# Linear attention with a gated feed-forward: the kernel's table of steps replaced by another

## Chip, cores, metric

The kernel runs on one NeuronCore of a Trainium2 chip. The metric is the device time of one execution in microseconds (us); lower is better. Three runs of the kernel before the change gave 242.40, 241.68 and 242.57 us, median 242.4.

## What is computed

Linear attention with phi(x) = elu(x) + 1 over q, k, v of shape (8 batches, 8 heads, 576 positions, 64), then a gated feed-forward over 4608 tokens, all float32 at the borders:

```python
q_p, k_p = (phi(q), phi(k))
kv = np.einsum('bhsd,bhse->bhde', k_p, v)
z = np.sum(k_p, axis=2)
num = np.einsum('bhsd,bhde->bhse', q_p, kv)
den = np.einsum('bhsd,bhd->bhs', q_p, z)[..., None] + 1e-06
attn = num / den
...
x = attn.transpose(0, 2, 1, 3).reshape(4608, 512)
a = x @ w1          # 512 x 1024
b = x @ w2          # 512 x 1024
h = a * b @ w3      # 1024 x 1024
return h @ w_out    # 1024 x 512
```

## The kernel before

**Work.** w3 and w_out are multiplied on the chip once, so that the end of the chain is one product with a 1024 x 512 matrix (wf). The 4608 tokens are 36 tiles of 128; four tiles make a chunk, and there are nine chunks, 0 to 8. Each chunk has eight gate units, one for 128 columns of w1 and w2: four matmuls of 512 columns for a, four for b, a copy of a to SBUF on ScalarE (ACT) and a product with b on VectorE (DVE). An output tile is eight matmuls over the eight units' results.

**Steps.** The program is a table of steps, `ORDER` (lines 21 to 60). Each entry calls one small function (`s_F`, `s_KV`, and so on, lines 133 to 562); the queues of all engines are filled in the order of the table, nothing is reordered afterwards, and an engine works off its queue strictly in that order. The last letter names the engine that copies: a is ACT, v is DVE, p is GpSimd (POOL), s is SyncE (SP). The steps that matter here:

- `LK LQ LV` load half a batch of k, q or v (576 KB); `L3 LH LO LA LB` load pieces of w3, w_out, w1 and w2 (512 KB, `LH` half of it). All these transfers are issued by SP, one after the other. They land in 13 buffers ("ld", line 96) that are given out first in, first out: the 14th load waits until the buffer that was first given back is read.
- `CO CA CB` cast a piece of w_out, w1 or w2 to bf16. `T3` and `C3` turn a block of w3, `FW` adds to wf.
- `EX`, `PT`, `PM` make phi: exp on ACT, max(x,0)+1 and the minimum of the two on DVE. `VC` casts v. `KV` and `KB` make kv for a batch.
- `QP` transposes phi(q) on TensorE (PE) through PSUM, with a copy back; `QD` does it as a DMA transpose between two SBUF tiles (line 385; ACT issues it when the letter is a, else SP).
- `ND` makes one tile of normalised attention: products on PE, then reciprocal and multiplication on DVE. `NT` with three `NM` does it for three tiles with one reciprocal.
- `XP` (PE and a copy) or `XD` (DMA transpose, SP) turn these tiles round for the gate units.
- `F` is a whole gate unit; `FI` one side of it (a or b); `FP` one side for two of the four tiles, in the same PSUM buffer as the other two, which are read together; `FS` one side for two tiles in a PSUM buffer of its own, read by itself as 128x256.
- `O` is an output tile with its copy, `S` its store (two DMAs), `Q` the last tile in pieces.

**PSUM.** Four buffers ("mm") hold gate units and outputs, two ("at") the rest; each is free again when its copy is done.

**Stages.** First wf is made while weights and batch 0 arrive, then chunk 0 goes through its gate units as pieces of w1 and w2 arrive (units 0 to 3 need the first column half, 4 to 7 the second), then chunks follow one another with the output tiles of earlier chunks between them. In SBUF, w1 and w2 are cut as `w_part` says:

```python
    def w_part(w, x):
        if x > 5:
            return w[:, 2 * x - 12:2 * x - 10, 0:NCH]
        if x > 3:
            return w[:, :, P * (x - 4):P * (x - 3)]
        return w[:, :, 256 * x:256 * x + 256] if x < 2 else w[:, 2 * x - 4:2 * x - 2, NCH:DFF]
```

Pieces 6 and 7 are the two row halves of the first 512 columns; pieces 0 and 1 are columns 0 to 255 and 256 to 511 with all rows; 2 and 3 are the row halves of the second 512 columns.

Of the kernel before, what the change touches and what calls it, by code (L numbers as in the profile page):

```python
# [18 lines left out]


ORDER = """
I.0 H.3.0 L3.2 LO.0 I.1 T3.2.0.a H.1.1 CO.0.v FW.2.0.a T3.2.1.a H.1.2 LO.1 CO.1.a L3.4 T3.4.0.v
T3.4.1.v L3.3 T3.3.0.a LO.2 FW.4.0.v FW.4.1.a LO.3 L3.5 T3.3.1.v C3.5.a CO.2.v FW.2.1.a FW.2.2.a
CO.3.v FW.2.3.v L3.6 C3.6.v FW.3.0.a FW.3.1.v LK.0.0 T3.5.0.v LH.0.0 T3.5.1.v LQ.0.0 FW.4.2.v
EX.k.0.0 PT.k.0.0 FW.4.3.a EX.q.0.0 T3.6.0.v PM.k.0.0 FW.5.0.v FW.5.1.v L3.1 T3.6.1.a PT.q.0.0
PM.q.0.0 L3.7 FW.5.2.v FW.6.0.a FW.3.2.a FW.3.3.v FW.5.3.v LQ.0.1 T3.1.0.a C3.7.v T3.1.1.a FW.1.0.v
FW.1.1.a LK.0.1 PT.q.0.1 EX.q.0.1 PM.q.0.1 T3.7.0.a FW.6.1.v FW.6.2.a FW.6.3.a LV.0.0 I.2 T3.0.0.v
LV.0.1 EX.k.0.1 PT.k.0.1 T3.7.1.a LH.0.1 FW.7.0.a FW.7.1.v FW.1.2.v VC.0.0.v QP.0.0.v QP.0.1.a
FW.7.2.a KV.0.0.a PM.k.0.1 VC.0.1.v FW.7.3.v FW.1.3.a KV.0.1.v T3.0.1.a ND.0 FW.0.0.v LA.6 ND.1
FW.0.1.v CA.6.a LA.7 CA.7.a ND.2 FW.0.2.a XP.0.a XP.1.a ND.3 FW.0.3.a FP.0.0.0.0 LB.6 LQ.1.1  # L30
EX.q.1.1 LB.7 LA.3 XP.2.v XP.3.v FP.0.1.0.0 CB.7.a LA.2 FP.0.1.0.1 LB.3 PT.q.1.1 PM.q.1.1 FI.0.2.0
FI.0.3.0 CB.6.v FI.0.1.1 LB.2 CA.2.a LQ.1.0 CB.3.v FP.0.0.0.1 FI.0.0.1 FI.0.3.1 CB.2.v QP.1.1.v
CA.3.a PT.q.1.0 LK.1.0 FI.0.2.1 PT.k.1.0 EX.q.1.0 PM.q.1.0 F.0.4 EX.k.1.0 PM.k.1.0 F.0.5 LV.1.0
VC.1.0.a F.0.6 LK.1.1 EX.k.1.1 PT.k.1.1 PM.k.1.1 LV.1.1 LK.3.0 KV.1.0.a VC.1.1.a F.0.7 LQ.3.1
QP.1.0.a KV.1.1.v PT.k.3.0 EX.q.3.1 EX.k.3.0 O.0.a LQ.3.0 EX.q.3.0 PT.q.3.1 ND.4 ND.5 O.1.a XP.4.a
ND.6 ND.7 PM.k.3.0 LK.2.0 XP.5.a O.2.a PM.q.3.1 XP.6.v XP.7.v LQ.2.1 EX.k.2.0 LQ.2.0 PT.k.2.0
PM.k.2.0 PT.q.3.0 EX.q.2.0 LK.3.1 PM.q.3.0 O.3.a LV.4.1 F.1.0 LV.2.0 LK.4.1 S.0.s F.1.1 PT.q.2.1
EX.q.2.1 S.1.s PT.k.3.1 F.1.2 EX.k.3.1 PM.k.3.1 LK.2.1 PM.q.2.1 F.1.3 VC.2.0.a LV.2.1 PT.k.2.1
PT.q.2.0 PM.q.2.0 EX.k.2.1 F.1.4 LV.3.0 F.1.5 VC.2.1.a PM.k.2.1 F.1.6 LV.3.1 VC.3.0.v QD.2.1
EX.k.4.1 KB.2.a QD.2.0 VC.3.1.a ND.8 QD.3.0 F.1.7 KB.3.a NT.9 NM.9.0 NM.9.1 QD.3.1 XD.2.0 NM.9.2  # L40
XD.2.1 S.2.s LK.4.0 O.4.v O.5.v NT.12 LV.4.0 NM.12.0 O.6.v NM.12.1 O.7.v NM.12.2 LQ.4.1 PT.k.4.0
F.2.0 F.2.1 F.2.2 F.2.3 F.2.4 EX.k.4.0 PT.k.4.1 LQ.5.1 F.2.5 PM.k.4.1 F.2.6 VC.4.0.a LQ.4.0 VC.4.1.a
PM.k.4.0 F.2.7 S.3.s S.4.s LQ.5.0 LK.5.1 PT.q.5.0 EX.q.5.0 NT.15 PM.q.5.0 EX.q.4.1 NM.15.0 PT.q.4.1
PM.q.4.1 PT.q.4.0 LQ.7.1 S.5.s KB.4.a PT.k.5.1 O.8.v EX.k.5.1 S.6.s LK.5.0 EX.k.5.0 PT.k.5.0 XD.3.0
XD.3.1 O.9.a O.10.a O.11.v LV.5.1 F.3.0 PM.k.5.1 LK.6.0 F.3.1 PM.k.5.0 EX.q.4.0 NM.15.1 NM.15.2
LV.5.0 S.7.s S.8.s LK.6.1 F.3.2 S.9.s S.10.s VC.5.0.v PM.q.4.0 QD.4.0 EX.k.6.0 QD.4.1 F.3.3 F.3.4
EX.q.5.1 PT.q.5.1 PM.q.5.1 PT.k.6.1 F.3.5 F.3.6 F.3.7 QD.5.1 O.12.v NT.18 QD.5.0 NM.18.0 XD.4.0
NM.18.1 VC.5.1.a PT.k.6.0 KB.5.a XD.4.1 LQ.6.1 O.13.a O.14.v PT.q.7.1 O.15.v F.4.0 EX.q.7.1 PM.q.7.1
F.4.1 F.4.2 NM.18.2 LK.7.0 F.4.3 NT.21 EX.k.6.1 NM.21.0 NM.21.1 NM.21.2 LV.6.0 VC.6.0.v F.4.4 F.4.5
S.11.s S.12.s PT.k.7.0 LK.7.1 LQ.7.0 F.4.6 LV.6.1 VC.6.1.v S.13.s S.14.s F.4.7 PT.q.7.0 PM.k.6.1  # L50
LQ.6.0 PM.k.6.0 O.16.v EX.q.7.0 O.17.v PM.q.7.0 PT.q.6.1 LV.7.0 O.18.v XD.5.0 XD.5.1 EX.q.6.1
PM.q.6.1 LV.7.1 VC.7.0.a S.15.s EX.q.6.0 KB.6.a NT.24 O.19.v NM.24.0 PT.q.6.0 PM.q.6.0 QD.6.1 F.5.0
VC.7.1.v EX.k.7.1 PT.k.7.1 F.5.1 F.5.2 EX.k.7.0 NM.24.1 NM.24.2 QD.7.1 PM.k.7.0 F.5.3 F.5.4 QD.6.0
PM.k.7.1 F.5.5 S.16.s S.17.s NT.27 XD.6.0 NM.27.0 NM.27.1 QD.7.0 KB.7.a NM.27.2 F.5.6 XD.6.1 XD.7.0
F.5.7 S.18.s NT.30 S.19.s O.20.v S.20.s F.6.0 NM.30.0 NM.30.1 NM.30.2 F.6.1 XD.7.1 O.21.v NT.33
O.22.v NM.33.0 NM.33.1 O.23.v F.6.2 F.6.3 F.6.4 F.6.5 F.6.6 F.6.7 F.7.0 F.7.1 F.7.2 F.7.3 F.7.4
F.7.5 F.7.6 S.21.s S.22.s S.23.s XD.8.0 NM.33.2 XD.8.1 O.24.a O.25.v O.26.v O.27.v S.24.s S.25.s
S.26.s S.27.s F.7.7 F.8.0 F.8.1 F.8.2 F.8.3 F.8.4 F.8.5 F.8.6 F.8.7 O.28.a O.29.a O.30.a S.28.s
S.29.s S.30.s O.31.v S.31.s O.32.v S.32.s O.33.v S.33.s O.34.a S.34.b Q.35
"""  # L60


# [540 lines left out]
```

## Time and profile before

| | |
|---|---|
| median of three runs | 242.4 us (241.68 to 242.57) |
| the profiled execution | 241.85 us, of which 240.1 us from the first to the last instruction (the span) |
| PE busy | 230.6 us, 96% of the span, 2227 matmuls |
| DVE, ACT, POOL busy | 158.2, 113.9, 1.3 us |
| moved by DMA | 55.79 MB; the 16 DMA engines are full for the first 70 us |
| granted TensorE clock | 0.997 |

Times inside the execution count from the first instruction. A matmul's end is modelled, so PE's busy time includes the run-out of each burst. An engine's idle time costs only if the chain that ends last passes through it.

### The profile page before, as it was taken

To read this page: it belongs to the slowest core of one execution; us is meant where nothing else is said; L and a number is where in the kernel's file an instruction comes from. 1 tells how busy PE (TensorE), PEld (TensorE's weight loads), DVE (VectorE), ACT (ScalarE), POOL (GpSimd) and SP (SyncE) were. 2 spreads that over 40 slices of the span, in tenths; PEclk is the share of its full clock that TensorE was granted. 3 is DMA by queue.
4 is the path that set the end of the run, shared out by engine and by line. 5 is a ranking of instruction groups with operands and counts; after the bars stand their busy time and mean duration, and the time that the engine had idled before them with its cause. 6 is when DMAs were issued, how large, how long until landed. Compare 5 with 4: busy or idle time off the path is not lost.

```text
span 240.1 us, 5470 instructions
## 1 busy us (share of the span) xinstructions
PE 230.6 (96%) x2227; PEld 115.8 (48%) x2246; DVE 158.2 (66%) x287; ACT 113.9 (47%) x166; POOL 1.3 (1%) x9
## 2 busy tenths in 40 slices
...
DMA  6999999999998999989959998795653001700276
GB/s 245 418 376 405 387 387 390 388 391 389 397 272 155 183 362 360 319 195 317 257 111 279 381 369 211 123 202 111 137 120 83 3 0 44 163 15 0 45 155 149
DMA packets 52040, 55.79 MB, mean 232 GB/s; under 512 B 31280, under 2 KB 31536, under 8 KB 52016
## 3 DMA queue, kind: packets, MB, share of 16 engines
...
q8 instruction: 17, 0.28, 0.5%
...
## 4 chain that ended last, share of the span: by engine, by line
PE 90%; DMA 5%; DVE 1%; issue 1%; SPq 1%; ACT 0%
PE a_ps L482 26%; PE b_ps L482 26%; PE o_ps L535 24%; PE wf_ps L263 6%; DMA w<-in_moe_w_dram 3%; PE nd L398 2%; DMA qt<-phq 2%; PE w3p L251 2%; PE kbp L340 1%; PE qp L368 1%; PE xp L457 1%; PE kvp L340 1%; DVE w3t L252 1%; SPq L157 1%; DVE xt L458 0%
## 5 line engine op out<-in xcount | busy, mean ns | idle before, releaser
L482 PEld LDWEIGHTS <-w_sb 128*128 128x128 bf16 x584 | 56.4, 98 | 66.9 <-issue 0.9
L491 ACT COPY a_sb<-a_ps 128x512 f32<-128x512 f32 x72 | 42.1, 585 | 80.9 <-PE a_ps L482 79.0
L493 DVE TENSOR_TENSOR ab<-a_sb,b_ps 128x512 bf16<-128x512 f32 x72 | 49.1, 686 | 39.3 <-PE b_ps L482 37.5
L482 PE MATMUL a_ps<-xt,w_sb 128*128 128x512 bf16 (+1 forms) x296 | 74.0, 374 | 0.1
L482 PE MATMUL b_ps<-xt,w_sb 128*128 128x512 bf16 x288 | 73.8, 380 | 0.0
L535 PE MATMUL o_ps<-wf_sb,ab 128*128 128x512 bf16 (+2 forms) x290 | 63.5, 368 | 1.2 <-issue 0.6
L535 PEld LDWEIGHTS <-ab 128*128 128x128 bf16 x304 | 28.3, 98 | 31.2
L542 DVE COPY o_sb<-o_ps 128x512 f32<-128x512 f32 x23 | 15.9, 690 | 20.6 <-PE o_ps L535 19.5
L404 DVE TENSOR_TENSOR xn<-nd,r 128x512 bf16<-128x512 f32 (+2 forms) x45 | 24.3, 578 | 0.5
L273 ACT ACTIVATE eq<-q 128x1152 bf16<-128x1152 f32 x16 | 18.4, 1163 | 6.1 <-DVE phk L293 3.1
L273 ACT ACTIVATE ek<-k 128x1152 bf16<-128x1152 f32 x16 | 18.7, 1167 | 2.0 <-DMA k<-in_k_dram 1.9
L263 PE MATMUL wf_ps<-wo_sb,w3t 128*128 128x512 bf16 x59 | 15.7, 384 | 1.7 <-DVE wo_sb L217 1.0
L542 ACT COPY o_sb<-o_ps 128x512 f32<-128x512 f32 x12 | 7.0, 580 | 15.7 <-PE o_ps L535 15.7
L293 DVE TENSOR_TENSOR phq<-phq,eq 128x1152 bf16<-128x1152 bf16 x16 | 12.0, 752 | 1.4 <-ACT eq L273 0.9
L285 DVE TENSOR_SCALAR phq<-q 128x1152 bf16<-128x1152 f32 x16 | 12.1, 753 | 0.8 <-DMA q<-in_q_dram 0.8
L285 DVE TENSOR_SCALAR phk<-k 128x1152 bf16<-128x1152 f32 x16 | 12.1, 753 | 0.1
L293 DVE TENSOR_TENSOR phk<-phk,ek 128x1152 bf16<-128x1152 bf16 x16 | 12.0, 752 | 0.2
L327 ACT CAST vt<-v 128x1152 bf16<-128x1152 f32 x9 | 10.3, 1159 | 0.0
L398 PEld LDWEIGHTS <-qt 64*64 64x64 bf16 x576 | 6.3, 106 | 5.2 <-issue 3.0
L263 PEld LDWEIGHTS <-w3t 128*128 128x128 bf16 x64 | 5.6, 98 | 6.5 <-issue 1.5
L398 PE MATMUL nd<-kv,qt 64*64 64x65 bf16 x576 | 8.2, 194 | 0.5 <-DMA qt<-phq 0.5
L251 PE MATMUL w3p<-ident,w 128*128 128x128 f32 x40 | 6.9, 307 | 1.4 <-DMA w<-in_moe_w_dram 1.0
...
## 6 DMA issues: line engine op xcount, KB each, us to landing
...
wa<-in_moe_w_dram SPq DMA_DIRECT2D x4, 512.0 KB, 11.0
wb<-in_moe_w_dram SPq DMA_DIRECT2D x4, 512.0 KB, 11.0
```

Source lines behind the costliest of these rows:

```text
L251: nc.tensor.transpose(tp[:, c, :], blocks[:, 2 * x + c // 2, c % 2, :], idt)
L263: nc.tensor.matmul(wfs[i], w3ts[i][:, c, :], wo_sb[:, c, :], start=(c == 0), stop=(c == FC - 1))
L273: nc.scalar.activation(out=t, in_=raw[n, b, h], func=AF.Exp)
L285: (nc.gpsimd if e == "p" else nc.vector).tensor_scalar(out=by_set(n, t), in0=by_set("k", raw[n, b, h]), scalar1=0.0, scalar2=1.0, op0=ALU. ...
L293: nc.vector.tensor_tensor(out=t, in0=t, in1=by_set("k", es[n, b, h]), op=ALU.min)
L398: nc.tensor.matmul(dst[g * R:(g + 1) * R], qts[b, a // 2][rows, j, a % 2 * R:(a % 2 + 1) * R], kvs[b][rows, a // 2, a % 2, :], start=True, ...
L404: nc.vector.tensor_tensor(out=xn[:, :, a0:a1], in0=n4[:, :, :, 0:D], in1=r.unsqueeze(3).to_broadcast([P, 2, a1 - a0, D]), op=ALU.mult)
L482: nc.tensor.matmul(ops_[key][:, tiles.start * P:tiles.stop * P], w[:, w_row(kc), f * P:(f + 1) * P], xts[c0][:, tiles, kc, :], start=(kc = ...
L491: nc.scalar.copy(out=a_sbs[c0, f], in_=ops_[key])
L493: nc.vector.tensor_mul(out=abs_[c0][:, f, :], in0=a_sbs[c0, f], in1=ops_[key])
L535: nc.tensor.matmul(o_ps, abs_[c0][:, f, m * P:(m + 1) * P], wf_sb[:, f, cols], start=(f == 0), stop=(f == FC - 1))
L542: copy_of(e)(out=o_sbs[t], in_=o_ps)
```

## The change

Only the table differs; the functions are the same (they stand one line lower, L221 is L222, since the table is a line longer). What the new table does:

- **w1's first column half** is loaded and cast as pieces 1 and 0 (column quarters) in place of 6 and 7 (row halves), and w2's piece 7 comes first. Rows of 1 KB take the place of rows of 2 KB in two transfers.
- **The first four gate units** of chunk 0 are 16 `FS` steps in place of four `FP` and six `FI`.
- **q of batch 1** is turned by two `QD` steps issued from ACT in place of `QP` (18 transposes on PE, one copy on DVE and one on ACT).
- **Tiles 0 to 2** are normalised by `NT` with three `NM` in place of three `ND`.
- **Six weight casts** go to GpSimd: one of w_out, three of w1, two of w2. Before, all fifteen casts of weights (with `C3`) were on ACT or DVE.
- The first loads are in another order (w3 blocks 4 and 1 first, block 0 in halves before q), and the steps of the later batches and chunks are shuffled: outputs stand between the gate units of chunk 3, for one thing.

A line of the old table and one of the new, from the first gate units:

```diff
-FW.0.1.v CA.6.a LA.7 CA.7.a ND.2 FW.0.2.a XP.0.a XP.1.a ND.3 FW.0.3.a FP.0.0.0.0 LB.6 LQ.1.1
...
+FS.0.2.1.0 CA.2.a CB.3.v QD.1.1.a FS.0.1.1.1 LQ.3.0 PT.q.1.0 F.0.4 EX.q.1.0 PM.q.1.0 F.0.5 PT.k.1.0
```

What POOL has in its queue before, in the stage that loads weights (`ident` is the identity for transposes, `vt` the cast v with its column of ones):

```order
masks.py:197 MEMSET ident_68 128x128
masks.py:199 ISA
masks.py:199 AFFINE_SELECT ident_68<-ident_68 128x128
L138 CAST ident<-ident_68 128x128
L141 MEMSET vt_74 128x36
L141 MEMSET vt_75 128x36
```

And with the change:

```order
L139 CAST ident<-ident_68 128x128
L218 CAST wo_sb<-wo 128x1024
L142 MEMSET vt_74 128x36
L142 MEMSET vt_75 128x36
L222 CAST w_sb<-wa 128x4x256 x2
L227 CAST w_sb<-wb 128x2x512
L222 CAST w_sb<-wa 128x2x512
L227 CAST w_sb<-wb 128x2x512
```

Six casts have come in, one of `wo` (w_out) ahead of the memsets and five of `wa` and `wb` (w1 and w2) behind them, one after the other.

ACT's queue around the last pieces of chunk 0 and batch 1, before (`a_sb` is a gate unit's a, `eq` and `ek` the exponentials, `kv` the batch's kv):

```order
L491 COPY a_sb<-a_ps 128x512
L273 ACTIVATE ek<-k 128x1152
L491 COPY a_sb<-a_ps 128x512
L327 CAST vt_75<-v 128x18x64
L491 COPY a_sb<-a_ps 128x512
L273 ACTIVATE ek<-k 128x1152
L348 CAST kv<-kvp 128x130
L327 CAST vt_75<-v 128x18x64
L491 COPY a_sb<-a_ps 128x512
L369 COPY qt<-qp 128x1152
```

And with the change:

```order
L521 COPY a_sb<-a_ps 128x256 x4
L222 CAST w_sb<-wa 128x2x512
L386 DMA_TRANSPOSE qt<-phq 128x9x128
L492 COPY a_sb<-a_ps 128x512
L274 ACTIVATE eq<-q 128x1152
L492 COPY a_sb<-a_ps 128x512
L274 ACTIVATE ek<-k 128x1152
L386 DMA_TRANSPOSE qt<-phq 128x9x128
L492 COPY a_sb<-a_ps 128x512 x2
L274 ACTIVATE ek<-k 128x1152
L328 CAST vt_75<-v 128x18x64
L349 CAST kv<-kvp 128x130
```

The copy `qt<-qp` is gone, two DMA transposes stand in the queue, the second one ahead of the copies of units 6 and 7, and one of the two casts of v has left for DVE.

SP's queue around the transposes for chunk 4 (`qt<-phq` is `QD`, `xt<-xn` is `XD`, `out_dram` a store), before:

```order
L548 DMA out_dram<-o_sb 64x512 x4
L385 DMA_TRANSPOSE qt<-phq 128x9x128 x4
L462 DMA_TRANSPOSE xt<-xn 128x8x128 x2
L157 DMA q<-in_q_dram 128x2x576
L157 DMA k<-in_k_dram 128x2x576
```

And with the change:

```order
L158 DMA q<-in_q_dram 128x2x576
L386 DMA_TRANSPOSE qt<-phq 128x9x128 x2
L463 DMA_TRANSPOSE xt<-xn 128x8x128
L549 DMA out_dram<-o_sb 64x512 x8
L463 DMA_TRANSPOSE xt<-xn 128x8x128
L386 DMA_TRANSPOSE qt<-phq 128x9x128 x2
```

Eight stores now stand between the two transposes that feed chunk 4.

More of the change, by code (lines that the diff above doesn't have):

```diff
@@ L33 @@
[L33 to L38, printed above, removed]
@@ new lines @@
+C3.5.v I.2 FW.4.3.v LK.0.0 FW.1.2.v FW.1.3.v T3.7.0.a T3.7.1.a FW.0.2.a QP.0.0.a LV.0.0 T3.5.0.v
+FW.0.3.v FW.7.0.v FW.7.1.a FW.7.2.a EX.k.0.1 T3.2.0.a PT.q.0.1 FW.7.3.a T3.2.1.a T3.3.0.a T3.5.1.a
+L3.6 FW.5.0.v LV.0.1 LB.7 LA.1 CA.1.p LA.0 PT.k.0.0 EX.q.0.1 LB.6 PM.q.0.1 FW.3.0.a FW.2.0.v
+FW.2.1.a T3.3.1.a PT.k.0.1 PM.k.0.1 EX.k.0.0 FW.2.2.a PM.k.0.0 LQ.1.1 C3.6.v FW.2.3.v VC.0.0.a LA.3
+QP.0.1.a FW.5.1.a FW.5.2.v FW.3.1.v FW.5.3.a KV.0.0.v VC.0.1.v FW.3.2.a CA.0.p T3.6.0.a T3.6.1.v
+FW.3.3.v CB.6.p LA.2 LB.2 KV.0.1.a NT.0 NM.0.0 FW.6.0.a LB.3 FW.6.1.a FW.6.2.a CB.7.a LQ.1.0 NM.0.1
@@ new lines @@
+NM.0.2 FW.6.3.a XP.0.a XP.1.v LK.1.0 ND.3 XP.2.a FS.0.2.0.0 LV.1.0 FS.0.3.0.0 FS.0.1.0.0 PT.q.1.1
+XP.3.a CA.3.p FS.0.0.0.0 FS.0.0.1.0 LK.1.1 LV.1.1 EX.q.1.1 FS.0.1.1.0 FS.0.2.0.1 FS.0.3.0.1
+FS.0.2.1.1 PM.q.1.1 FS.0.1.0.1 FS.0.3.1.1 LK.2.1 CB.2.p FS.0.0.0.1 FS.0.0.1.1 FS.0.3.1.0 LK.2.0
+FS.0.2.1.0 CA.2.a CB.3.v QD.1.1.a FS.0.1.1.1 LQ.3.0 PT.q.1.0 F.0.4 EX.q.1.0 PM.q.1.0 F.0.5 PT.k.1.0
+VC.1.0.v EX.k.1.0 PM.k.1.0 PT.k.1.1 QD.1.0.a F.0.6 F.0.7 KV.1.0.v EX.k.1.1 PM.k.1.1 O.0.v VC.1.1.a
+KV.1.1.a ND.4 ND.5 LQ.2.0 EX.k.2.1 O.1.a XP.4.a ND.6 ND.7 EX.q.3.0 PT.k.2.1 XP.5.a LK.3.1 O.2.a
```

58 lines of the change are left out of this document (27 added, 31 removed).

## The prediction

> **What bounds the kernel now.** I read the busy times first, then cut the span into stages, then followed the chain of waits through them.
>
> ```profile
> PE 230.6 (96%) x2227; PEld 115.8 (48%) x2246; DVE 158.2 (66%) x287; ACT 113.9 (47%) x166; POOL 1.3 (1%) x9
> DMA  6999999999998999989959998795653001700276
> ```
>
> PE is busy nearly always, and the DMA engines are full in the first 11 to 13 of 40 slices (6 us each). The same by stages (columns: stretch, its length, busy time of PE, PEld, DVE, ACT, POOL, granted clock, DMA share, GB/s):
>
> ```profile
> 0.00:10.86 10.86, 8.33 (x32) 5.83 (x33) 2.26 (x4) 3.40 (x4) 1.35 (x9) 1.00 0.82 323
> 10.86:30.55 19.69, 18.19 (x188) 10.71 (x188) 15.36 (x25) 11.51 (x16) 0.00 (x0) 1.00 1.04 391
> 30.55:42.69 12.14, 11.68 (x137) 6.69 (x139) 9.99 (x22) 10.16 (x14) 0.00 (x0) 1.00 1.05 389
> 42.69:59.99 17.30, 17.09 (x224) 8.88 (x225) 15.74 (x33) 15.95 (x21) 0.00 (x0) 1.00 1.05 389
> 59.99:84.31 24.32, 23.64 (x351) 11.72 (x353) 21.51 (x40) 13.81 (x21) 0.00 (x0) 1.00 1.02 253
> 84.31:236.70 152.39, 151.63 (x1303) 71.97 (x1311) 93.10 (x164) 59.10 (x91) 0.00 (x0) 1.00 0.66 174
> 236.70:240.07 3.37, 0.00 (x0) 0.00 (x0) 0.29 (x1) 0.00 (x0) 0.00 (x0) 0.79 0.56 156
> ```
>
> I cut at the first unbroken run of wf products (10.86), the first normaliser (30.55), gate unit 4 of chunk 0 (42.69), chunk 1 (59.99), chunk 2 (84.31) and the last matmul (236.70). PE idles 2.5, 1.5, 0.5, 0.2, 0.7, 0.8 and 3.4 us in them. The reader should see how little is left: from 30.55 to the last matmul 2.1 us. A new order of the same work can win little there and can lose any amount, so each stage is priced by what may make PE wait.
>
> **The start: about +0.6 us.** A w_out piece cast on GpSimd stands ahead of the first wf product.
>
> ```profile
> 8.76 1.21 PE L251 MATMUL w3p<-ident,w 128*128 128x128 f32 x8 [0.97 <-DMA w<-in_moe_w_dram]
> L138 POOL CAST ident<-ident 128x128 bf16<-128x128 f32 x1 | 0.3, 289 | 0.1
> L587 POOL MEMSET const-float32-1.0<- 128x1 f32 x1 | 0.1, 98 | 0.0
> L226 DVE CAST w_sb<-wb 128x1024 bf16<-128x1024 f32 x3 | 2.1, 687 | 0.0
> L221 ACT CAST w_sb<-wa 128x1024 bf16<-128x1024 f32 x4 | 4.1, 1051 | 0.0
> L251 PE MATMUL w3p<-ident,w 128*128 128x128 f32 x40 | 6.9, 307 | 1.4 <-DMA w<-in_moe_w_dram 1.0 <-DVE w3t L252 0.3
> L263 PE MATMUL wf_ps<-wo_sb,w3t 128*128 128x512 bf16 x59 | 15.7, 384 | 1.7 <-DVE wo_sb L217 1.0 <-issue 0.5 <-ACT w3t L252 0.2
> L148 PE MATMUL warm<-zero 128*128 128x256 f32 x10 | 4.6, 600 | 1.2 <-DVE zero L135 1.2
> ```
>
> By the first row the fourth transfer has landed at 8.7. Before it is a block of w3; with the change it is w_out's piece 0. A 1024-column cast on POOL is in no row. Bounds: not under DVE's 0.69 us, not over eight times the 128-column cast, 2.3 us. I take the slope between the two POOL rows, (289 - 98) / 128 = 1.49 ns a column, hence 0.1 + 1.5 = 1.6 us. The product starts at 10.3, 0.5 earlier than the run at 10.86, but with more left: four float32 transposes (0.17 each), two products (0.27) and two warming matmuls (0.46), 2.1 us. Against it, the wait of 1.0 us for a w_out cast (the row of L263, "DVE wo_sb") may go. -0.5 + 2.1 - 1.0 = +0.6, with -0.4 if PE's first work hides all of the difference, and +1.6 if that wait stays.
>
> **The first gate units: +0.1.**
>
> ```profile
> L432 DVE RECIPROCAL r<-r 128x24 f32<-128x24 f32 x9 | 2.7, 303 | 0.3
> L404 DVE TENSOR_TENSOR xn<-nd,r 128x512 bf16<-128x512 f32 x27 | 18.5, 687 | 0.5
> L404 DVE TENSOR_TENSOR xn<-nd,r 128x384 bf16<-128x384 f32 x9 | 4.9, 549 | 0.0
> L404 DVE TENSOR_TENSOR xn<-nd,r 128x128 bf16<-128x128 f32 x9 | 2.5, 282 | 0.0
> L491 ACT COPY a_sb<-a_ps 128x512 f32<-128x512 f32 x72 | 42.1, 585 | 80.9 <-PE a_ps L482 79.0 <-DVE ab L493 1.1
> L357 ACT CAST kv<-kbp 128x130 bf16<-128x130 f32 x12 | 2.6, 270 | 4.3 <-PE kbp L340 4.3
> L482 PE MATMUL a_ps<-xt,w_sb 128*128 128x256 bf16 x16 | 2.4, 272 | 0.1
> 42.85 0.86 PE a_ps L482 x4
> 50.28 0.50 PE qp L368 x9
> 19.16 1.63 SPq L157 DMA_DIRECT2D wa<-in_moe_w_dram  x2
> 28.82 2.15 SPq L157 DMA_DIRECT2D wb<-in_moe_w_dram  x2
> DMA to landing us min/median/max: 11.0/11.0/11.1
> ```
>
> Three tiles in one visit delay the first two: reciprocal 0.30, then 0.69 + 0.55 + 0.28 on DVE before tile 1 can be turned, 1.8 us where two single visits let the first tile go after 0.9. PE covers most of it with eight wf products (8 x 0.27 = 2.2 us) that stand behind; I leave +0.4. The half-width matmuls stream the same columns: four of 512 take 0.86 (chain row), so one of 256 should take 0.11; the 256-column row has 2.4 / 16 = 0.15 with its run-outs, so 64 of them cost between 0 and 2.6 us more. Bursts follow one another here, so I take 0.2. ACT's copies at 256 columns are 0.27 + 126 x 0.82 ns = 0.37, eight for four of 0.585: +0.65 us, off PE's path. One transposition of q (0.50) leaves. +0.4 + 0.2 - 0.5 = +0.1, so unit 4 starts at 42.69 + 0.7 = 43.4. The floor: the last piece of w2 (second issue of the row at 28.82) is issued at 30.2 and lands 11.0 later, at 41.2, behind the same bytes in both tables; with a cast of 0.69 its b side cannot start before 41.9, so at most 0.8 us can be won up to here. The casts that leave ACT and DVE free those engines, not PE, and count nothing.
>
> The third of w1's loads now waits for the buffer that POOL's first w1 cast reads. That piece is the 21st transfer, the second issue of the row at 19.16 (20.4): it lands at 31.5 and is read by 33.1. Four transfers of 1.4 us are still under way then, to about 37: hidden, unless a cast takes over 3 us. The 1 KB rows I cost at nothing; the bytes are the same, and half the row could cost up to a fifth of 2.6 us, which the range holds.
>
> **q of batch 1 by DMA: +0.6.**
>
> ```profile
> L369 ACT COPY qt<-qp 128x1152 bf16<-128x1152 bf16 x2 | 2.2, 1118 | 1.0 <-PE qp L368 1.0
> 114.84 5.70 SPq L385 DMA_TRANSPOSE qt<-phq  x4
> DMA to landing us min/median/max: 3.2/3.5/5.2
> 45.00:50.00 5.00, 5.00 (x59) 2.34 (x57) 4.70 (x8) 4.92 (x8) 0.00 (x0) 1.00 1.05 391
> 75.00:80.00 5.00, 4.95 (x160) 2.83 (x154) 4.12 (x10) 0.44 (x2) 0.00 (x0) 1.00 0.96 125
> L273 ACT ACTIVATE ek<-k 128x1152 bf16<-128x1152 f32 x16 | 18.7, 1167 | 2.0 <-DMA k<-in_k_dram 1.9
> 48.94 1.17 ACT L327 CAST vt<-v 128x1152 bf16<-128x1152 f32 x1
> 53.03 0.38 PE nd L398 x32
> ```
>
> ACT gives up 1.12 us of copy and takes 2 x 1.43 us of issue, in a stretch where it is 98% busy (4.92 of 5). What is queued behind the second issue are the copies of units 6 and 7, for which PE's buffers wait only when four are taken: one unit of slack, 1.7 us. SP's loads share their completion counters with the two transposes, so a later load waits for each landing; with 11 us from issue to landing at 1.5 us a load some seven are in flight, so the engines don't run dry. The larger price is DMA time. At 75 to 80, nearly all transposes, the engines were full at 125 GB/s; at 45 to 50, loads, full at 391. A half of q is 128 x 1152 x 2 bytes = 0.295 MB: 2.3 us of all engines, 4.5 us for both, put among the loads that batch 1 itself waits for. v's second half is cast at 48.94 now, as it lands; it comes 0 to 4.5 us later. The first transpose surely goes ahead of it. The second is issued after two copies and two exps (0.585 and 1.17 each) from the end of unit 4's a side, 43.4 + 0.9 + 3.5 = 47.8, when v is nearly through; I take 2.3. Then v lands at 51.2, is cast at 52.4, and kv and its copy end at 53.1. The second transpose lands at 51.3 if alone (3.5), at 58.8 if it stands behind a full queue as loads do (11). The nearest row is the slowest transpose, 5.2, which had loads ahead of it; here loads also run beside it, up to another 2.3: between 53.0 and 55.3, I take 54.2. The first tile that needs it comes at 54.3 instead of 53.03: +1.3. PE alone would be there at 53.03 + 0.7 - 0.5 = 53.2, so PE waits about a microsecond here, where it waited for nothing.
>
> The Trainium skill (DMA: Bandwidth & Descriptors, Queues, rings and completion order) says that each DMA engine takes turns between the queues that have work, a packet at a time; by it the second transpose takes 1.4 us of issue and twice 2.3 of transfer, lands at 53.8, and the sum would be 0.4 lower. No row of before shows two queues at work at once.
>
> **Chunks 1 to 8: +0.4.**
>
> ```profile
> 57.93:76.06 18.13, 18.13 (x289) 9.11 (x286) 16.99 (x29) 15.71 (x23) 0.00 (x0) 1.00 1.06 301
> 93.40 2.41 SPq L548 DMA_DIRECT2D out_dram<-o_sb  x4
> ```
>
> Between the normalisers of tile 7 and of tile 9, DVE has 16 halves of phi instead of 14 (+1.5 us) and two turning copies less (-0.8). It has 1.1 us of room there by the first row, so 0; without that room +0.7. In chunks 2 to 8 the matmuls are the same. Eight stores at 0.6 us (second row) stand between the two token transposes of chunk 4, 4.8 us: the second lands between 0 and 0.7 us after PE is ready; I take 0.4. The tail is the same.
>
> **Sum.** 0.6 + 0.1 + 0.6 + 0.4 = +1.7 on the profiled execution's 241.85 us (span 240.1 and 1.75 around it): 243.55. The median of the runs, 242.4, is 0.55 above that execution; I go half of the way and forecast **243.8 us**.
>
> **Rivals.** *PE's own path decides*: the transposes slip between the loads, the first tile of batch 1 comes at 53.2, the start costs -0.4 instead of +0.6, nothing is late in chunk 4: -0.4 + 0.1 - 0.5 = -0.8, and another -0.5 if chunk 1's wait for a transposed q goes: 241.85 - 1.3 + 0.3 = 240.9. For it: no late stage has slack to lose, and PE has less to do by 1.0 us. *The second transpose lands behind the loads*: at 57 the first tile is 4.1 us late instead of 1.3: 246.6. It decides from a landing at 54.3 on; for it speaks that loads take 11 us to land there, against it that a transpose is on a queue of its own. *GpSimd is slower than its small row*: five casts in a row from 31.5; at 2.5 us each the last ends at 44.0, just when unit 4's b side wants it; from there every 0.1 us costs 0.5, so 3 us each, 46.5, give 246.0. *GpSimd and DVE hold each other up*: phi's minimum, with two operands in SBUF, stands still until the last POOL cast ends, and the w2 cast and unit 4 behind it: half a cast, 0.8 us: 244.6. *The change doesn't do what it says*: casts and transposes are hidden wherever they are and PE's order is as good: 242.4.
>
> The Trainium skill (SBUF — State Buffer, Who interferes with whom) has the fourth rival as a rule: a DVE instruction in a two-port mode or with two SBUF inputs and a GpSimd one share ports, and the later waits. No row of before shows POOL beside such an instruction.
>
> **How the numbers follow.** Forecast (243.0 to 245) 0.35, PE's path 0.20, late transpose 0.20, slow GpSimd 0.08, shared ports 0.07, nothing happens 0.10. The range is 240.8 to 247.2: it reaches from the first rival's time past the late transpose's, and leaves out slower GpSimd casts and the far ends. About 0.5% (1.2 us) is what a measurement can tell from no change: faster than 241.2 has most of the first rival, 0.17; within, the rest of it, the last and a third of the forecast, 0.28; slower 0.55.
>
> **What would show it.** Right: POOL casts of 1.4 to 1.8 us; unit 4 of chunk 0 at 43 to 44; a PE wait of about 1 us "<-DMA qt" ahead of the first tile of batch 1; chunk 2 at 85 to 86. Wrong: chunk 1 before 60.0 with no such wait; casts over 2.5 us; a DVE minimum of over 1 us beside a POOL cast; a wait over 1 us after chunk 2, which I found no cause for.

## The result

The changed kernel takes 248.22 us (247.49 to 248.93, four runs) beside 242.43 us for the kernel before on the same chip (four runs): a ratio of 1.024, interval 1.021 to 1.028. It is 5.8 us slower; I had forecast 243.8 and a range up to 247.2.

The busy times of the changed kernel, and PE's busy tenths in 40 slices, first of the kernel before and then of the changed one:

```profile
PE 229.6 (93%) x2232; PEld 118.5 (48%) x2252; DVE 148.9 (60%) x273; ACT 118.7 (48%) x178; POOL 7.6 (3%) x15
PE   7789999999999899999999999999999999999994
PE   3999999936999899999999999999999999999994
```

PE has 1.0 us less to do, and yet the span is 6.7 us longer (246.8 for 240.1). The hole is one place, the ninth and tenth slice, 49 to 62 us; the 3 at the front is the wait for the first data, which before was filled with warming matmuls. The same by stages, cut at unit 4 of chunk 0 (41.96), the first tile of batch 1 (54.76), chunk 1 (65.68), chunk 2 (90.50) and the last matmul:

```profile
41.96:54.76 12.80, 9.61 (x114) 4.58 (x112) 9.52 (x16) 6.54 (x8) 0.00 (x0) 1.00 1.09 341
54.76:65.68 10.92, 8.18 (x125) 4.48 (x116) 6.06 (x16) 5.95 (x10) 0.00 (x0) 0.84 1.09 352
65.68:90.50 24.82, 23.60 (x350) 11.64 (x352) 21.21 (x41) 15.14 (x21) 0.00 (x0) 1.00 0.96 221
90.50:243.27 152.77, 151.98 (x1303) 71.88 (x1311) 88.30 (x157) 64.93 (x101) 0.00 (x0) 1.00 0.68 176
```

| stage | before | after | difference | predicted |
|---|---|---|---|---|
| to unit 4 of chunk 0 | 42.69 | 41.96 | -0.7 | +0.7 |
| unit 4 to chunk 1 | 17.30 | 23.72 | +6.4 | +0.6 |
| chunk 1 | 24.32 | 24.82 | +0.5 | 0 |
| chunks 2 to 8 | 152.39 | 152.77 | +0.4 | +0.4 |
| behind the last matmul | 3.37 | 3.53 | +0.2 | 0 |

In the second stage PE idles 5.9 us where it idled 0.2. PE's timeline has the three waits (start, length, and in brackets the idle time before it and what ended that):

```profile
51.87 1.89 PE L536 MATMUL o_ps<-wf_sb,ab 128*128 128x512 bf16 x7 [2.43 <-ACT a_sb L492]
54.46 0.48 PE L341 MATMUL kvp<-vt,phk 64*64 64x65 bf16 x36 [0.71 <-ACT vt L328]
57.30 0.65 PE L399 MATMUL nd<-kv,qt 64*64 64x65 bf16 x31 [2.35 <-DMA qt<-phq]
```

The first two have one cause. ACT's timeline, with its queue's DMA issues:

```profile
40.47 1.38 ACTq L386 DMA_TRANSPOSE qt<-phq  x1
45.72 5.42 ACTq L386 DMA_TRANSPOSE qt<-phq  x1
51.23 1.08 ACT L492 COPY a_sb<-a_ps 128x512 f32<-128x512 f32 x2 [4.79 <-issue]
```

The second transpose's issue holds ACT for 5.42 us, not 1.4; the two copies behind it are those of units 6 and 7, and v's cast comes after them. The third wait is for the transpose itself. The rows of DMA issues give 14.3 us from issue to landing for the first half and 11.5 for the second, so they land at 54.8 and 57.2:

```profile
qt<-phq ACTq DMA_TRANSPOSE x1, 14.3
...
qt<-phq ACTq DMA_TRANSPOSE x1, 11.5
```

Why so late, the DMA queues say. In the stretch from 48 to 50 us (packets, MB, share of 16 engines; q1 is SP's queue, q10 ACT's):

```profile
q1 hardware_dynamic: 317, 0.69, 88.4%
q10 hardware_dynamic: 318, 0.08, 18.0%
```

One packet of ACT's queue goes for each packet of SP's. A load packet has 2304 bytes, a transpose packet 256, so the transposes get every other packet and a tenth of the bytes.

The packets are not all of the 14.3 us. The first half's first packet moves at 44.5, 4.1 us after the issue began; its 1152 packets are through at about 53.4, after two pauses (from 45.5 and from 50.0); it lands at 54.8. The second half goes mostly behind 54, and faster, because by then few loads run beside it. SP has issued none for 9.3 us: by the profile its next load waits for the first half to land. SP's timeline and waits, and the queues from 55 to 56 us:

```profile
45.05 10.13 SPq L158 DMA_DIRECT2D q<-in_q_dram  x2
SPq L158 <- DMA qt<-phq: 9.3, 1, 9.3
q10 hardware_dynamic: 413, 0.11, 120.0%
q1 hardware_dynamic: 25, 0.04, 11.4%
```

### The profile page after: what moved, and what is told of

Read it like the earlier page. It is cut to its first block, busy times and chain, and to the rows that moved or that the text cites. A ratio compares the mean times of both kernels' runs of the same rounds, so it can differ in the third digit from the quotient of the medians.

```text
span 246.8 us, 5484 instructions
## 1 busy us (share of the span) xinstructions
PE 229.6 (93%) x2232; PEld 118.5 (48%) x2252; DVE 148.9 (60%) x273; ACT 118.7 (48%) x178; POOL 7.6 (3%) x15
## 4 chain that ended last, share of the span: by engine, by line
PE 74%; DMA 17%; ACT 2%; DVE 2%; issue 2%; SPq 2%; ACTq 0%
PE a_ps L483 23%; PE o_ps L536 23%; PE b_ps L483 22%; DMA qt<-phq 5%; DMA wa<-in_moe_w_dram 4%; DMA wo<-in_moe_w_out_dram 4%; DMA k<-in_k_dram 3%; PE nd L399 2%; DMA xt<-xn 2%; PE kbp L341 1%; PE wf_ps L264 1%; SPq L158 1%; ACT w3t L253 1%; DVE phk L294 1%; ACT eq L274 0%
## 5 line engine op out<-in xcount | busy, mean ns | idle before, releaser
L483 PEld LDWEIGHTS <-w_sb 128*128 128x128 bf16 x544 | 52.6, 98 | 63.2 <-DMA xt<-xn 0.6
L494 DVE TENSOR_TENSOR ab<-a_sb,b_ps 128x512 bf16<-128x512 f32 x68 | 46.4, 686 | 51.8 <-PE b_ps L483 47.3
L483 PE MATMUL a_ps<-xt,w_sb 128*128 128x512 bf16 x272 | 69.9, 379 | 0.1
L483 PE MATMUL b_ps<-xt,w_sb 128*128 128x512 bf16 x272 | 69.8, 379 | 0.0
L492 ACT COPY a_sb<-a_ps 128x512 f32<-128x512 f32 x68 | 39.7, 586 | 60.9 <-PE a_ps L483 53.2
L536 PE MATMUL o_ps<-wf_sb,ab 128*128 128x512 bf16 (+2 forms) x288 | 65.2, 371 | 3.7 <-ACT a_sb L492 2.4
L543 ACT COPY o_sb<-o_ps 128x512 f32<-128x512 f32 x22 | 12.9, 587 | 40.4 <-PE o_ps L536 40.4
L543 DVE COPY o_sb<-o_ps 128x512 f32<-128x512 f32 x13 | 9.0, 690 | 7.6 <-PE o_ps L536 7.6
L328 ACT CAST vt<-v 128x1152 bf16<-128x1152 f32 x8 | 9.3, 1158 | 0.0
L252 PEld LDWEIGHTS w3p<-ident,w 128*128 128x128 f32 x40 | 6.6, 209 | 5.3 <-issue 4.6
```

What stands on the lines that cost most here:

```text
L252: nc.tensor.transpose(tp[:, c, :], blocks[:, 2 * x + c // 2, c % 2, :], idt)
L483: nc.tensor.matmul(ops_[key][:, tiles.start * P:tiles.stop * P], w[:, w_row(kc), f * P:(f + 1) * P], xts[c0][:, tiles, kc, :], start=(kc = ...
L492: nc.scalar.copy(out=a_sbs[c0, f], in_=ops_[key])
L494: nc.vector.tensor_mul(out=abs_[c0][:, f, :], in0=a_sbs[c0, f], in1=ops_[key])
L536: nc.tensor.matmul(o_ps, abs_[c0][:, f, m * P:(m + 1) * P], wf_sb[:, f, cols], start=(f == 0), stop=(f == FC - 1))
L543: copy_of(e)(out=o_sbs[t], in_=o_ps)
```

## The experiments

**Theory A**: the whole loss sits in the two DMA transposes. A1 says how: two queues take turns packet by packet, so small packets advance at the pace of large ones, and an issue waits for room in its queue. A2 and A3 are rivals on the same part (any transpose beside loads holds ACT; the price is the transposes' own DMA time). **Theory B**: the rest of the new order loses too. Time ratios are to the kernel before, run on the same chip beside each set.

**1. Both halves by PE again.**

```diff
-FS.0.2.1.0 CA.2.a CB.3.v QD.1.1.a FS.0.1.1.1
+FS.0.2.1.0 CA.2.a CB.3.v QP.1.1.v FS.0.1.1.1
-PT.k.1.1 QD.1.0.a F.0.6 F.0.7
+PT.k.1.1 F.0.6 F.0.7 QP.1.0.a
```

> The changed kernel with both halves of batch 1's q turned by PE again (first half copied by DVE, second by ACT, the second after unit 7 as in the kernel before); everything else of the change stays. Theory A (the whole loss sits in the two DMA transposes on ScalarE's queue): unit 4 of chunk 0 stays at 42.0, chunk 1 begins at 59.3 to 59.8 instead of 65.7, the time is 241.6 to 242.4. Theory B (the other parts lose as well, the new order of chunks 1 to 8 or the GpSimd casts): chunk 1 begins near 60, but the time stays at 243.5 or more.

Measured: 243.39 us, ratio 1.002 (0.998 to 1.006; the kernel before took 243.31 in this set): the loss is gone. Chunk 1 begins at 61.35, later than A said, though, and the time is 1 us over its range (the kernel before is itself 0.9 us slower in this set than beside the result). PE's timeline shows a wait that the transposes had covered:

```profile
53.57 0.48 PE L341 MATMUL kvp<-vt,phk 64*64 64x65 bf16 x36 [1.06 <-ACT vt L328]
```

**2. Only the first half by DMA**: the second of the two edits above alone.

> The changed kernel with only the first half of batch 1's q by DMA from ScalarE's queue; the second half is turned by PE. Theory A1 (packets of the two queues take turns one for one, and the second issue has to wait for room that the first one leaves): the first half still lands 11 to 14 us after its issue, at 52 to 55, but ScalarE is never held for over 1.5 us by an issue; PE waits at most 1.5 us ahead of batch 1; 242.0 to 243.7. Theory A2 (any DMA transpose beside loads holds ScalarE): an issue of 4 us or more stays, and the time is 246 or more.

Measured: 244.56, ratio 1.007 (1.002 to 1.012). The half lands 13.7 us after its issue and the issue takes 1.36 us; PE waits 0.54 us for it. So a transpose beside loads is slow even when alone, but an issue into an empty queue holds nobody: A1, not A2. The time is 0.9 over A1's range, as in the first experiment, whose late v and whose set it shares.

**3. Both on SP's queue.**

```diff
-QD.1.1.a
+QD.1.1
-QD.1.0.a
+QD.1.0
```

> The changed kernel with both DMA transposes issued by SP, at the same places of the order, so behind the loads of SP's own queue. Theory A1 (turns between two queues): in one queue the transposes go in order, so the first lands 8 to 11 us after its issue, at 49 to 51, the second near 56; ScalarE is not held, its copies of units 6 and 7 come on time; PE still waits 1 to 3 us for the second half: 244 to 246.5. Theory A3 (the price is the transposes' DMA time itself, whatever the queue): 247.5 to 249, as now.

Measured: 249.82, ratio 1.028 (1.023 to 1.033), nearest to A3's time and 0.8 over it. The order was A1's: the transposes go in order with the loads, ACT is never held. But SP is, as its timeline shows, with PE's below it:

```profile
42.05 7.28 SPq L386 DMA_TRANSPOSE qt<-phq  x1
50.05 2.79 SPq L386 DMA_TRANSPOSE qt<-phq  x1
```

```profile
57.68 0.65 PE L399 MATMUL nd<-kv,qt 64*64 64x65 bf16 x31 [5.42 <-DMA qt<-phq]
```

Its queue was full of loads, the first issue took 7.28 us, and the second could not be issued before 50. That the first waited for room in the queue is my reading: the profile names a DVE instruction (k's phi) as what ended the wait, which the transpose does not read, and the count of packets in the last section speaks for room. The halves land at 53.7 and 57.6 and PE waits in one piece. I had counted the order in a queue and forgotten its length.

**4. The kernel before with only the transposes**: `QP.1.1.v` becomes `QD.1.1.a` in its place, `QP.1.0.a` becomes `QD.1.0.a` behind unit 5.

> The kernel before with only this part of the change: both halves of batch 1's q by DMA from ScalarE's queue, the second issued after unit 5. Theory A (the transposes alone make the loss): 247 to 250, with an issue of 4 us or more on ScalarE and chunk 1 at 65 to 67. Theory B (it takes the other parts too): 242 to 244.5.

Measured: 247.04, ratio 1.017 (1.012 to 1.021), so A, with chunk 1 at 65.4 and this issue on ACT (PE then waits 3.3 us for v's cast behind it):

```profile
46.25 3.62 ACTq L384 DMA_TRANSPOSE qt<-phq  x1
```

**5. Small load packets beside the transposes.** Of five loads the columns come in quarters of 288 elements, which are columns of other rows; bytes and work stay the same:

```diff
     def head_rows(src, b, h):
+        if (src, b, h) in [(k, 1, 1), (v, 1, 1), (k, 2, 1), (k, 2, 0), (q, 3, 0)]:
+            return src[b].rearrange("h (p j) d -> (h p) (j d)", j=J).rearrange(
+                "(g p) x -> p g x", p=P)[:, :, h * HW // 4:(h + 1) * HW // 4]
```

> The changed kernel with five of the loads that run beside the two transposes (k and v second half of batch 1, k of batch 2, q of batch 3) fetched as 1152-byte pieces instead of 2304-byte ones: the same bytes in twice the packets, out of columns that belong to other rows of the head, so the output is not the reference's; the work is the same. Theory A1 (one packet of ScalarE's queue for one of SP's): the transposes' packets come faster, 220 or more a us instead of 160 while both queues are at work, the first half lands 9 to 12 us after its issue instead of 14.3, the second issue holds ScalarE for 2 to 4 us instead of 5.4, and the time falls by 1 to 4 us, to 244 to 247. Theory A3 (the transposes have a rate of their own): still about 160 a us, 14 us, and 248 or more, with the loads no faster.

Measured: the packets did as A1 says. The same stretch, 48 to 50 us:

```profile
q1 hardware_dynamic: 529, 0.59, 82.2%
q10 hardware_dynamic: 535, 0.14, 30.1%
```

268 transpose packets a us for 159, still one for one; the first half lands after 10.8 us for 14.3, and the second issue takes 2.27 us for 5.42 (the first, into an empty queue, 2.24). That settles turns by packets against a rate of the transposes' own. The time did not follow: 248.10, ratio 1.023 (1.019 to 1.026). The second half still lands at 56.3, 10.4 us after its issue: here loads stay beside it (267 of their packets from 54 to 55, where the changed kernel had 114). PE waits 3.92 us for it in one piece instead of 2.4 and 2.4 in two. The held ACT had been hidden behind the late landing.

**6. Only the second half by DMA** (the first of the edits of experiment 1 alone).

> The changed kernel with only the second half of batch 1's q by DMA from ScalarE's queue; the first half is turned by PE and copied by DVE. ScalarE's queue holds nothing when the transpose is issued at 45 to 46, so the issue takes 1.4 us and the copies of units 6 and 7 come on time. Theory A1: packet for packet beside loads it still lands 11 to 14 us later, at 57 to 59, and PE waits 3 to 5 us for it in one piece: 247 to 249, as slow as with both. Rival (the held ScalarE is the price): without the hold PE waits under 2 us, 244 to 245.5.

Measured: 250.74, ratio 1.034 (1.030 to 1.037), slower than with both. The issue takes 1.36 us, the landing 13.2:

```profile
59.45 0.65 PE L399 MATMUL nd<-kv,qt 64*64 64x65 bf16 x31 [7.04 <-DMA qt<-phq]
```

The rival is out: without any hold it is worse, by 2 us more wait than A1 said. The first packet moves at 50.3, 4.1 us after the issue, 1088 of the 1152 are through by 56.5, and the rest take until 59 in a pause in which both queues nearly stop, at 80 GB/s from 56.5 to 58:

```profile
DMA packets 111, 0.12 MB, mean 80 GB/s; under 512 B 62, under 2 KB 62, under 8 KB 111
```

In the changed kernel the second half's packets follow the first's without that start.

**7. The GpSimd casts back on DVE and ACT**, on top of experiment 1 (`CO.0.p CB.6.p CB.2.p` to v, `CA.1.p CA.0.p CA.3.p` to a, each in its place).

> The kernel with both halves turned by PE (first experiment), and its six weight casts back from GpSimd: CO.0, CB.6 and CB.2 on DVE, CA.1, CA.0 and CA.3 on ScalarE. If the GpSimd casts (1.04 us each in the profile of the changed kernel) gain or cost something, it is at the start and in the first gate units: theory C (they are hidden either way): within 0.6 us of the first experiment. Rival (they take load off engines that bound the first gate units): slower by 1 to 2 us. Rival (they disturb DVE): faster by 0.5 to 1.5 us.

Measured: 254.57, ratio 1.051 (1.047 to 1.054), outside all three. ACT's timeline has the reason:

```profile
31.68 1.04 ACT L222 CAST w_sb<-wa 128x1024 bf16<-128x1024 f32 x1 [7.11 <-DMA wa<-in_moe_w_dram]
32.63 1.16 ACT L274 ACTIVATE eq<-q 128x1152 bf16<-128x1152 f32 x1
```

The table has that cast early, and on ACT it waits 7.1 us for its load with q's exponential behind it; PE waits 7.6 us for q, and 2.0 us at the start for w_out's cast on DVE. On GpSimd, which has nothing else to do, the same early place costs nothing. What the GpSimd casts give this order is a queue in which an instruction may wait.

**8. Experiment 1 with q's second copy on DVE** (`QP.1.0.a` becomes `QP.1.0.v`).

> The first experiment with the second half's copy on DVE instead of ScalarE. In the first experiment ScalarE copies q at 50.3 to 51.4 and only then works on k's exponential and v's cast, for which PE waits 1.1 us (and 0.3 for kv) ahead of batch 1's first tile, while DVE idles 1.3 us. With the copy on DVE the first tile should come about 1 us earlier, at 52.7 to 53.2, chunk 1 at 60.2 to 60.6: 242.2 to 242.8 beside 243.4, a little under the kernel before. If something else is late next (DVE's own k minimum, v's landing) the gain is under 0.4 us.

Measured: 242.01, ratio 0.999 (0.996 to 1.002); the first tile comes at 52.9, chunk 1 at 60.4. This takes away what experiment 1 had left, and it is the best version here; it can't be told from the kernel before.

**9. The kernel before with six casts on GpSimd** (`CO.0 CA.6 CA.7 CB.6 CA.3 CB.2` to p).

> The kernel before with six weight casts on GpSimd and nothing else changed: CO.0, CA.6, CA.7, CB.6, CA.3, CB.2, each in its old place of the order. GpSimd takes 1.04 us for one where DVE takes 0.69 and ScalarE 1.05. Theory C (the casts are off PE's path; what GpSimd's queue gives in the changed kernel is only a place where a cast can wait for its load without holding others): the order before never holds an engine on these six, so 242.0 to 242.8, no difference. Rival (time taken off DVE and ScalarE is worth something by itself in the first gate units): 241.2 to 241.9. Rival (GpSimd beside DVE slows DVE): 243 to 244.

Measured: 242.59, ratio 1.002 (0.9995 to 1.004): theory C, no difference.

**10. Experiment 8 with the warming matmuls ahead of the first product.**

```diff
-I.0 I.1 L3.4 T3.4.0.v T3.4.1.a L3.1 H.3.0 T3.1.0.a T3.1.1.v LO.2
+I.0 H.3.0 I.1 L3.4 T3.4.0.v T3.4.1.a L3.1 T3.1.0.a T3.1.1.v H.3.1 LO.2
-FW.4.0.a H.1.2 LQ.0.0 ... L3.7 H.1.1 L3.5
+FW.4.0.a LQ.0.0 ... L3.7 L3.5
```

> The previous best version (both halves of q by PE, the second copied by DVE) with the ten warming matmuls of the start placed where PE waits for data: three (six records) ahead of the first transposes, three between w3's second block and the first wf product, and none in the stretch from 10.4 on, where PE is the bound. In the changed kernel two pairs stand behind 10.4 and take 0.43 us each. If PE is the bound from there, unit 4 of chunk 0 comes 0.5 to 0.9 us earlier, at 41.9 to 42.3, and the time is 241.2 to 241.6, under the kernel before. Rival (w_out's pieces bound the start, so PE just waits where it warmed): no gain, 242.0.

Measured: 242.89, ratio 1.002 (0.999 to 1.005). The rival: a wait of 0.88 us for w_out's cast by ACT stands where the warming was, and unit 4 comes at 42.5.

**11. Transposes on SP's queue, ahead of three loads.**

```diff
-LK.2.1 CB.2.p FS.0.0.0.1 FS.0.0.1.1 FS.0.3.1.0 LK.2.0
+CB.2.p FS.0.0.0.1 FS.0.0.1.1 FS.0.3.1.0
-QD.1.1.a FS.0.1.1.1 LQ.3.0
+QD.1.1 FS.0.1.1.1
-PM.q.1.0 F.0.5
+PM.q.1.0 QD.1.0 LK.2.1 LK.2.0 LQ.3.0 F.0.5
-PT.k.1.1 QD.1.0.a
+PT.k.1.1
```

> The changed kernel with both DMA transposes on SP's queue, and the three loads that stood ahead of the second (k of batch 2, first half of q of batch 3) moved behind it. What the earlier runs showed of one queue is used: it works in order, and an issue waits for room. Only the four loads that batch 1 needs are ahead of the first transpose, so it should land at 50 to 52, right behind v's second half, the second at 52 to 54; ScalarE's queue issues nothing. Then PE waits at most 1 us for a transposed q, chunk 1 begins at 59.3 to 60.5, and the time is 241 to 242.8, with 1.0 us of transposes taken off PE. Rival (the three loads come 4 to 6 us later and their exponentials are missed in chunk 1, or SP's issue is held for so long that the DMA engines run dry): chunk 1 in time but 243 to 245. If transposes are slow in any queue at work: 247 or more.

Measured: 245.89, ratio 1.015 (1.011 to 1.019). The place was right: the halves land at 51.2 and 52.1, PE's first tile of batch 1 is earlier than in the kernel before. The rival took the gain; the time is 3.1 us over the range and 0.9 over the rival's. PE's timeline, and ACT's ahead of that copy:

```profile
52.12 0.45 PE L399 MATMUL nd<-kv,qt 64*64 64x65 bf16 x31 [0.62 <-DMA qt<-phq]
60.20 1.89 PE L536 MATMUL o_ps<-wf_sb,ab 128*128 128x512 bf16 x8 [2.63 <-ACT xt L459]
```

```profile
58.52 1.16 ACT L274 ACTIVATE eq<-q 128x1152 bf16<-128x1152 f32 x1 [2.54 <-DVE phk L286]
```

The row names DVE, but the exponential waits only for its load and for a buffer whose reader was done at 45.4 us. The load is issued at 50.6 and lands 7.5 us later, at 58.1; in experiment 1 it is issued at 42.0 and lands at 54.0. The stretch from 47 to 52 us of this kernel, and of experiment 8, has the price (packets, MB, mean; the next row counts the small ones with it):

```profile
DMA packets 2472, 0.91 MB, mean 182 GB/s; under 512 B 2330, under 2 KB 2330, under 8 KB 2471
```

```profile
DMA packets 904, 1.95 MB, mean 391 GB/s; under 512 B 59, under 2 KB 59, under 8 KB 903
```

2330 packets of 256 bytes are 0.60 MB, so loads got 0.31 MB here and 1.95 MB there: 1.64 MB less, 4.2 us at 391 GB/s. Only a part of that is the transposes' own traffic. The two issues hold SP from 40.07 to 49.39, so that no load is issued meanwhile, and in two places of the stretch the engines do little (the last two figures are DMA share and GB/s); the last row is the us from 49 to 50:

```profile
40.07 9.32 SPq L386 DMA_TRANSPOSE qt<-phq  x2
48.50:49.00 0.50, 0.50 (x32) 0.26 (x34) 0.50 (x2) 0.50 (x2) 0.00 (x0) 1.00 0.22 48
50.25:51.00 0.75, 0.75 (x7) 0.21 (x6) 0.64 (x1) 0.47 (x1) 0.00 (x0) 1.00 0.22 13
DMA packets 946, 0.24 MB, mean 243 GB/s; under 512 B 945, under 2 KB 945, under 8 KB 945
```

At 945 packets a us the 2304 of both halves need 2.4 us by themselves. Of the rest of the 4.2, about 1 us is the two gaps (0.78 of 1.25 us); where the remainder lies I did not settle. The rival's second half, SP held until they run dry, fits that; no run separates the two.

**12. The second issue behind the copies of units 6 and 7**: `QD.1.0.a F.0.6 F.0.7` becomes `F.0.6 F.0.7 QD.1.0.a`, nothing else of the change is touched.

> The changed kernel with the second transpose's issue behind the copies of units 6 and 7 on ScalarE's queue, nothing else moved. If the held ScalarE is the price, taking the copies out from behind it gains 2 to 3 us: 245 to 246. If the landing of the second half is the price (it now starts 2 to 4 us later, though in room that the first half has left by then), the wait of 2.4 us for the copies goes and comes back as a longer wait for q: 247.5 to 250, no better than the changed kernel.

Measured: 249.03, ratio 1.029 (1.025 to 1.033). The landing is the price: the wait for the copies is gone and this stands in its place:

```profile
58.05 0.65 PE L399 MATMUL nd<-kv,qt 64*64 64x65 bf16 x31 [4.18 <-DMA qt<-phq]
```

**13. Experiment 11 with late exponentials behind the copies.**

```diff
-ND.7 EX.q.3.0 PT.k.2.1
+ND.7 PT.k.2.1
-PT.k.2.0 PT.k.3.1 PT.q.2.0 S.0.s PM.k.2.1 XP.7.a PT.q.3.0 LQ.3.1 PM.q.3.0 EX.q.2.0 O.3.a F.1.0 EX.k.3.1 PM.q.2.0 F.1.1
+PT.k.2.0 S.0.s PM.k.2.1 XP.7.a PT.q.3.0 O.3.a EX.q.3.0 PM.q.3.0 F.1.0 PT.q.2.0 EX.q.2.0 PT.k.3.1 LQ.3.1 F.1.1 EX.k.3.1 PM.q.2.0
```

> The previous version (transposes on SP's queue ahead of three loads) with the exponentials of q of batches 3 and 2, and the minima of late loads, moved behind the copies of batch 1's turned tiles and the first units of chunk 1, so that no copy stands behind a load that lands at 58 to 61. If the rest of the loss in that version is only these late loads seen through ScalarE's order (PE waited 2.6 us for a copy behind an exponential that waited for its load), that wait goes, chunk 1 begins at 59.0 to 59.8, and the time is 241.0 to 243.0. Rival (the loads put off are needed so early that DVE and ScalarE can't catch up in chunk 1, or DMA transposes cost DMA time that is missed anyway): chunk 2 still at 87 or later, 244.5 to 246.

Measured: 246.47, ratio 1.016 (1.013 to 1.020), the rival, 0.5 over its range. Chunk 1 begins at 59.05, the earliest of all kernels, and the time comes back inside it; chunk 2 begins at 86.8 (84.3 before). PE's timeline, and ACT's ahead of it:

```profile
72.35 1.02 PE L482 MATMUL a_ps<-xt,w_sb 128*128 128x512 bf16 x4 [2.07 <-ACT a_sb L491]
```

```profile
70.66 1.16 ACT L273 ACTIVATE ek<-k 128x1152 bf16<-128x1152 f32 x1 [3.61 <-DMA k<-in_k_dram]
```

The wait has moved from the load of 58 us to the one of 70 us. From 52 us on, the DMA engines are full to about 75 (391 GB/s to 58, 395 to 64, 342 to 76). So I take it that DMA time lost before that is paid at some load; that this holds wherever the table puts the transposes is argued from these two placings, not tested further.

## Why the prediction was wrong

**The start, +0.6, and the first gate units, +0.1: wrong in size and sign, -0.7.** The first product comes at 10.11 (predicted 10.3). GpSimd's cast takes 1.04 us, less than my 1.6 (groups of the changed kernel, and below them its first two stages, cut at the first product, the first normaliser and unit 4):

```profile
L218 POOL CAST wo_sb<-wo 128x1024 bf16<-128x1024 f32 x1 | 1.0, 1042 | 7.4 <-DMA wo<-in_moe_w_out_dram 7.4
L222 POOL CAST w_sb<-wa 128x1024 bf16<-128x1024 f32 x3 | 3.1, 1040 | 24.2 <-DMA wa<-in_moe_w_dram 24.2
L227 POOL CAST w_sb<-wb 128x1024 bf16<-128x1024 f32 x2 | 2.1, 1042 | 1.9 <-DMA wb<-in_moe_w_dram 1.9
```

```profile
10.11:30.63 20.52, 19.69 (x196) 12.32 (x202) 13.93 (x23) 15.56 (x20) 0.31 (x2) 1.00 1.04 396
30.63:41.96 11.33, 10.84 (x175) 8.72 (x163) 8.39 (x21) 8.09 (x16) 5.20 (x5) 1.00 1.06 382
```

From the product to unit 4 PE is busy 30.5 us (29.9 before, from 10.86 on): 0.7 more, where my terms of work (2.1 - 0.5 + 0.2) made 1.8, and idle 1.3 for 2.0 us. The wait for w_out did go. The 1 KB rows, put at nothing, cost a tenth while they move: from 30 to 32 us, when 607 of 675 packets have 512 B to 2 KB, 352 GB/s for 390 in the kernel before. That is about 0.2 us of loads, and no wait of PE shows it. The slow-cast rival, which tipped at 2.5 us, is out; minima on DVE average 0.75 us as before, so nothing speaks for shared ports. Casts "count nothing": right in the kernel before (experiment 9), but in the new order their queue matters (experiment 7), which I had not looked for.

**q of batch 1 by DMA, +0.6: the step that failed, +6.4.** Five of its lines were wrong, the landing above all.

- *The landing, 54.2 taken, 57.2 measured.* I charged each half 2.3 us of DMA time and at most as much of loads beside it. By packets, a half has 1152 of them, and they go at 159 a us beside loads: 7.2 us for one half, and as much for the next one while loads last. On top come 4.1 us ahead of the first packet and the pauses, which no row of before had shown me. The Trainium skill (DMA: Bandwidth & Descriptors, Queues, rings and completion order) had the rule, and I quoted it: turns by the packet. The trace agrees (317 to 318, if what the profile counts as a packet is one of the page's), but I worked its sum out in bytes, 53.8, when in packets it says the opposite of what I took from it. The rival of a late second transpose named this landing with a chance of 0.20, for another reason (behind the loads), and its 246.6 lacked the held issue and the clock.
- *The issue, 1.43 us and one unit of slack.* 1.38 for the first, 5.42 for the second. The row that I read, four issues in 5.70 us, had none that took long, though other transposes of that kernel, those of tokens, took up to 3.48. By itself this would be covered by the landing: taking it away gains nothing (experiments 5, 6 and 12).
- *The DMA time, 2.3 us a half.* It came from the stretch of 75 to 80 us, which I called full at 125 GB/s. A share of 0.96 is a mean: cut into 40 slices, that stretch of the kernel before has gaps, and between them mostly 180 to 290 GB/s:

```profile
GB/s 92 20 14 10 10 125 279 289 291 279 11 0 0 8 141 221 221 223 203 203 213 201 201 184 207 103 29 133 0 29 197 268 272 229 37 8 10 10 8 10
```

By experiment 11 a half takes 1.2 us alone. That my 4.5 us for both is near the 4.2 lost there is luck, since those hold the gaps as well.

- *"The engines don't run dry."* The wait of SP for each landing was foreseen, its length of 9.3 us was not. The engines had the transposes to move, but the loads ran out from 54 to 57. I followed the price only to v and to the second half; the loads behind them pay it too (experiments 11 and 13). What SP's wait costs by itself no run separates.
- *PE alone "would be there at 53.2".* It slows when it waits. Behind the last wait the granted clock is 0.59:

```profile
57.30:61.00 3.70, 3.37 (x42) 1.79 (x43) 2.02 (x6) 0.00 (x0) 0.00 (x0) 0.59 1.03 386
```

That is 0.41 x 3.70 = 1.5 us. So 5.7 us more of idle time and 1.5 of clock, less 0.5 for the transposes that PE no longer does, make 6.7; 6.4 was measured, and where the other 0.3 went I did not settle.

**Chunks 1 to 8, +0.4: +0.9 measured, and where the size fits it is luck.** Chunk 1, put at 0, costs 0.5 more: it has a wait of 1.1 us ahead of a kv, where the kernel before had one of 0.5 us for a transposed q. Chunks 2 to 8 cost the 0.4, but not for my reason, a late transpose for chunk 4: no wait of over 0.2 us stands behind chunk 2, and the 0.4 lies in PE's busy time (151.98 us for 151.63). In which rows I did not settle.

**The chances and signs.** None of the four signs of being right came in the size given. By their own rule the chances make 0.25 within and 0.58 slower, not 0.28 and 0.55, and the 246.0 of slow GpSimd casts is counted from 243.55, where the other slower rivals are counted from 243.8.

What the experiments leave: undoing the transposes takes the loss away (1, 8), and making them alone brings most of it into the kernel before (4). The rest of the reshuffled order is worth nothing either way that can be measured. With the transposes landing in time, and three loads put behind them, 1.5% is still lost (11, 13): the late landing is not the whole price of doing them here.
